# mLSTM scan and feed-forward on one core: queries, keys and state as three bfloat16 parts in 120-row stacks that go through memory, from chunk 7 on

## The chip, the cores and the metric

The program runs on one core of a Trainium2 chip. The metric is the device time of one execution in microseconds, taken as the median of several runs.

## What is computed

For 4 batches and 8 heads, 768 tokens of 40 channels go through a gated matrix memory; its output, 3072 tokens of 320 channels, goes through a feed-forward layer with 2048 hidden units. Cut to what matters:

```python
for t in range(S):                                   # S = 768, D = 40
    m_new = np.maximum(f_gate[:, :, t] + m, i_gate[:, :, t])
    f_stab = np.exp(f_gate[:, :, t] + m - m_new)
    i_stab = np.exp(i_gate[:, :, t] - m_new)
    C = f_stab * C + i_stab * outer(v_t, k_t)         # 40 x 40 per batch and head
    n = f_stab * n + i_stab * k_t
    y[:, :, t] = sigmoid(o_gate_t) * (C @ q_t) / max(|n . q_t|, 1)
h = x @ w_in                                         # x: y as 3072 x 320
g = np.maximum(h, 0.0) + alpha * np.minimum(h, 0.0)
out = g @ w_out                                      # 3072 x 320
```

All inputs and the output are float32.

## The kernel before

**Chunks.** The scan is done in 24 chunks `n` of 128 tokens (6 per batch, `c = n % 6`), all 8 heads at a time. Within a chunk the kernel forms scores K·Q for each head (tile `pS`), multiplies them by decays `E`, and multiplies the result by the values (`pH`). What earlier chunks of the batch left is added from the state `C`, 40 rows (key channel) by 42 columns (values, two columns for the normalizer) per head: `from_state` (tile `pI`, line 299). `update_steps` (tile `pu`, line 151) adds a chunk's keys times values to the state.

**Steps.** `stage_a(n)` transposes the chunk's queries (`pq`) and keys (`pk`) so that channels stand on partitions (`transposed`, line 173, two heads per transpose in 104 rows: one head in rows 0 to 39, the other in rows 64 to 103), splits them into parts, updates the state and splits the values. `stage_b(n)` makes the two halves of the scores (even heads, odd heads), then state part, values and gates. `attention` weaves `stage_a(n+1)` with `stage_b(n)`. Chunks 0 to 6 use plain float32 (`NDIR = 7`).

**Parts.** From chunk 7 on, `stacked` makes a high and a low part, each in float32r (a form of float32 that one pass of the PE takes): ACT copies the high part out of PSUM (`qh`, `kh`, line 181), DVE or POOL subtracts (`ql`, `kl`, lines 183 and 185), and SP issues six copies of 40 rows (line 189) for the queries and six for the keys that lay the parts under each other in a stack of 120 rows (`qS`, `kS`). One matmul per head over the 120 rows then sums high·high, high·low and low·high (line 357). The state product uses the unsplit queries `qf` in float32, two heads at a time: the state tile has the even heads in rows 0 to 39 and the odd heads in rows 64 to 103, zeros elsewhere, so one matmul of 84 columns serves a pair.

**Feed-forward.** Twelve groups of 256 tokens (`FeedForward`): per pair of hidden tiles 16 matmuls of 256 columns into `ph` (lines 487 to 494), ACT and DVE apply the slope, ACT and POOL split the result (`gh`, `gl`, lines 509 and 510), 12 matmuls of 320 columns into `po` (line 518), two pairs later.

**Order.** Each engine runs its instructions in a fixed order. The program writes attention steps between feed-forward steps (`side.until`, 13 steps per group of two chunks); a scheduler in the framework then places every instruction on its engine, so a change of one part can move its neighbours. SP issues nearly all DMAs from one queue, in order: a DMA whose wait is not over holds back all behind it. Loads of `q`, `k`, `v` (`qn`, `kn`, `va`) and of the decay rows (`Lb`) are issued there two chunks ahead.

Of the kernel before, what the change touches and what calls it, by code (L numbers as in the profile page):

```python
# [17 lines left out]
def kernel(ctx: ExitStack, tc: tile.TileContext, q, k, v, i_gate, f_gate, o_gate, w_in, w_out, alpha, out):  # L18
# [54 lines left out]
    qn_t = [const.tile([P, H, 64], F32, tag=f"qn{i}", name=f"qn{i}") for i in range(NQ)]  # L73
    kn_t = [const.tile([P, H, 64], F32, tag=f"kn{i}", name=f"kn{i}") for i in range(NQ)]
# [4 lines left out]
    ones = const.tile([BH, R], F32, tag="ones", name="ones")  # L79
    eT = const.tile([P, NC, BH], F32, tag="eT", name="eT")  # L80
    gamB = const.tile([P, BH, NC], F32, tag="gamB", name="gamB")

    C_t = [const.tile([P, H, VA], F32, tag=f"C{i}", name=f"C{i}") for i in range(3)]
    L_d = dram.tile([BH, S], F32, tag="L_d", name="L_d")

    def load_qk(n):
        b, c = divmod(n, NC)
        t0 = c * P
        nc.sync.dma_start(qn_t[n % NQ][:, :, :D], q[b, :, t0 : t0 + P, :].rearrange("h p d -> p h d"))
        nc.sync.dma_start(kn_t[n % NQ][:, :, :D], k[b, :, t0 : t0 + P, :].rearrange("h p d -> p h d"))  # L90
# [34 lines left out]
    def weighed(n):  # L125
# [4 lines left out]
            kd, kn_t[n % NQ][:, :, :D], wT[:, c, b * H : (b + 1) * H].unsqueeze(2).broadcast_to([P, H, D]), ALU.mult  # L130
# [8 lines left out]
    def update_steps(n):  # L139
# [9 lines left out]
        for h in range(H):  # L149
            r = slice(64 * (h % 2), 64 * (h % 2) + D)  # L150
            nc.tensor.matmul(pu3[r, h], kd[:, h], va[:, h], start=True, stop=True)
        yield
        old, new = C_t[(n - 1) % 3], C_t[n % 3]
# [15 lines left out]

    def transposed(ps, src):  # L170
# [4 lines left out]
    def stacked(ps, nm, n, low, copy=None):  # L175


        X = sb.tile([3 * D, 2, 512], F32R, tag=f"{nm}S", name=f"{nm}S{n}")
        Xh = sb.tile([P, 512], F32R, tag=f"{nm}h", name=f"{nm}h{n}", bufs=1)
        Xl = sb.tile([P, 512], F32R, tag=f"{nm}l", name=f"{nm}l{n}", bufs=1)  # L180
        nc.scalar.copy(Xh[:R], ps[:R])
        if copy is not None and n in QLP:
            nc.gpsimd.tensor_tensor(Xl[:R], copy[:R], Xh[:R].bitcast(F32), ALU.subtract)
        else:
            nc.vector.tensor_tensor(Xl[:R], ps[:R], Xh[:R].bitcast(F32), ALU.subtract)
        for par in range(2):
            for j in range(3):
                src = (Xl if j == low else Xh)[64 * par : 64 * par + D]
                nc.sync.dma_start(X[j * D : (j + 1) * D, par].bitcast(F32), src.bitcast(F32))
# [899 lines left out]
```

## Time and profile before

| what | value |
|---|---|
| median of 3 runs | 517.41 us (514.90 to 520.62) |
| the profiled execution's own time | 514.52 us |
| its span | 512.8 us |
| mean granted PE clock | 0.992 of full |
| busy: PE, PE weight load | 494.3 us (96%), 479.7 us (94%) |
| busy: DVE, ACT, POOL | 338.5 us (66%), 306.3 us (60%), 242.0 us (47%) |
| DMA | 59.43 MB, 140,078 packets |

How to read it: PE is the matmul row, PEld its weight loads, which run beside matmuls. A matmul's row shows how long it is in flight; matmuls overlap, so what one costs is the distance from its start to the start of the next. A row of the timeline gives start and length in us, then engine, source line, operation, output tile <- input tiles, shapes and how many equal instructions it merges; in brackets the idle time before it and what ended it. "SPq" rows are SP issuing a DMA: their length is the time of issuing, not of the transfer. A float32 matmul appears as two records, since PE takes two passes over it; float32r and bfloat16 matmuls and transposes appear as one.

### The profile page before, as it was taken

Reading aid. Unit: us, or ns where it says so; the run is one execution under the profiler, and the core shown is the slowest. Engines: PE = TensorE matmul, PEld = TensorE weight load, DVE = VectorE, ACT = ScalarE, POOL = GpSimd, SP = SyncE. Lnnn points to the kernel's source line nnn. Section 1 sums busy time; section 2 is a strip of 40 time slices with the busy share of each in tenths; the row PEclk is TensorE's granted clock in tenths of the full one; section 3 lists DMA queues with packets and bytes.
Section 4 is the critical chain, followed back from the end, with each engine's and each line's share of the span. In section 5 each row is a group of like instructions: output and inputs, shape, how many; then the busy total and the mean of one; then the engine's idle time right before and its main releaser. Section 6 shows DMA issues by size and latency. Waiting matters only on the chain.

```text
span 512.8 us, 11517 instructions
## 1 busy us (share of the span) xinstructions
PE 494.3 (96%) x4319; PEld 479.7 (94%) x4319; DVE 338.5 (66%) x666; ACT 306.3 (60%) x635; POOL 242.0 (47%) x284
## 2 busy tenths in 40 slices
PE   8887999899999999999999999999999999999997
PEld 7766998889999999999899999998999999999996
DVE  7887999945544777773876667685686586552321
ACT  3768797753456566576785676567776563433332
POOL 6522334400267366564747556464765644333242
PEclk9997999999999999999999999999999999999999
DMA  9989996811175454367363464448343221000000
GB/s 170 229 180 260 256 242 171 170 27 38 60 175 132 117 145 109 99 168 147 85 167 109 116 144 117 119 119 179 102 126 91 71 71 41 1 27 0 27 1 26
DMA packets 140078, 59.43 MB, mean 116 GB/s; under 512 B 102824, under 2 KB 128440, under 8 KB 140024
## 3 DMA queue, kind: packets, MB, share of 16 engines
q1 hardware_dynamic: 139944, 58.61, 47.5%
q8 instruction: 34, 0.56, 0.5%
q14 instruction: 20, 0.16, 0.1%
q10 hardware_dynamic: 80, 0.11, 0.1%
HBM read 37.95 MB, written 4.03 MB: 82 GB/s over the span
## 4 chain that ended last, share of the span: by engine, by line
PE 75%; DVE 11%; DMA 4%; ACT 3%; issue 3%; SPq 2%; POOL 1%; ACTq 0%; DVEq 0%; POOLq 0%
PE po L518 28%; PE ph L487 4%; PE ph L494 4%; PE ph L488 4%; PE ph L490 4%; PE ph L491 4%; PE ph L489 4%; PE ph L492 4%; PE ph L493 4%; PE pI L299 3%; PE pH L282 3%; PE pS L357 2%; DMA og<-in_o_gate_dram 2%; SPq L112 1%; PE pk L173 1%
## 5 line engine op out<-in xcount | busy, mean ns | idle before, releaser
L510 POOL TENSOR_TENSOR gl<-g,gh 128x512 fp32r<-128x512 f32 x80 | 103.9, 1299 | 75.8 <-ACT gh L509 64.2
L518 PE MATMUL po<-OH,gh 128*128 128x320 f32 x384 | 116.3, 315 | 3.2 <-ACT gh L509 2.9
L518 PE MATMUL po<-OL,gh 128*128 128x320 f32 x384 | 113.9, 309 | 0.0
L500 DVE SCALAR_TENSOR_TENSOR g<-g,oma,ph 128x256 f32<-128x256 f32 x160 | 69.6, 476 | 64.4 <-ACT g L496 64.0
L496 ACT ACTIVATE g<-ph 128x512 f32<-128x512 f32 x96 | 57.5, 599 | 65.3 <-PE ph L494 51.6
L509 ACT CAST gh<-g 128x512 fp32r<-128x512 f32 x80 | 49.6, 620 | 52.5 <-DVE g L500 51.8
L518 PEld LDWEIGHTS po<-OH,gh 128*128 128x128 f32 x384 | 71.9, 188 | 4.4 <-ACT gh L509 3.6
L518 PE MATMUL po<-OH,gl 128*128 128x320 f32 x384 | 73.0, 312 | 0.0
L518 PEld LDWEIGHTS po<-OL,gh 128*128 128x128 f32 x384 | 72.0, 188 | 0.0
L346 ACT ACTIVATE E<-Lb,bT 128x128 f32<-128x128 f32 x176 | 54.6, 391 | 16.9 <-PE pH L282 12.8
L518 PEld LDWEIGHTS po<-OH,gl 128*128 128x128 f32 x384 | 59.6, 188 | 0.4 <-POOL gl L510 0.3
L487 PE MATMUL ph<-XH,WH 128*128 128x256 f32 x192 | 59.0, 307 | 0.3 <-DVE g L500 0.2
L488 PE MATMUL ph<-XH,WH 128*128 128x256 f32 x192 | 54.2, 282 | 0.0
L494 PE MATMUL ph<-X2L,W 128*128 128x256 f32 x192 | 54.1, 283 | 0.0
L489 PE MATMUL ph<-XH,WL 128*128 128x256 f32 x192 | 54.1, 282 | 0.0
L490 PE MATMUL ph<-XH,WL 128*128 128x256 f32 x192 | 53.9, 281 | 0.0
L491 PE MATMUL ph<-X,W 128*128 128x256 f32 x192 | 53.9, 281 | 0.0
L492 PE MATMUL ph<-XL,WH 128*128 128x256 f32 x192 | 53.8, 280 | 0.0
L493 PE MATMUL ph<-XL,WH 128*128 128x256 f32 x192 | 53.6, 279 | 0.0
L269 ACT CAST E<-pS 128x512 bf16<-128x512 f32 x64 | 37.5, 586 | 21.1 <-DVE pS L267 10.9
L349 POOL TENSOR_SCALAR_AFFINE_SELECT E<-E 128x512 f32<-128x512 f32 x44 | 30.6, 697 | 31.7 <-ACT E L346 22.8
L487 PEld LDWEIGHTS ph<-XH,WH 128*128 128x128 f32 x192 | 36.3, 189 | 1.2 <-DVE g L500 0.5
(168 smaller groups left out, 1095.9 us busy)
## 6 DMA issues: line engine op xcount, KB each, us to landing
Lb<-L_d SPq DMA_DIRECT2D x22, 512.0 KB
qS<-qh SPq DMA_DIRECT2D x68, 80.0 KB
kS<-kh SPq DMA_DIRECT2D x68, 80.0 KB
wo<-in_moe_w_out_dram SPq DMA_DIRECT2D x8, 640.0 KB
wi<-in_moe_w_in_dram SPq DMA_DIRECT2D x8, 512.0 KB
qn<-in_q_dram SPq DMA_DIRECT2D x24, 160.0 KB
kn<-in_k_dram SPq DMA_DIRECT2D x24, 160.0 KB
va<-in_v_dram SPq DMA_DIRECT2D x24, 160.0 KB
```

The lines of the kernel that those rows point to most:

```text
L487: nc.tensor.matmul(dst, WH[half][:, 0, hs], XH[:, 0], start=True, stop=False)
L488: nc.tensor.matmul(dst, WH[half][:, 1, hs], XH[:, 1], start=False, stop=False)
L489: nc.tensor.matmul(dst, WL[half][:, 0, hs], XH[:, 0], start=False, stop=False)
L490: nc.tensor.matmul(dst, WL[half][:, 1, hs], XH[:, 1], start=False, stop=False)
L491: nc.tensor.matmul(dst, W2[:, fs], X2, start=False, stop=False)
L492: nc.tensor.matmul(dst, WH[half][:, 0, hs], XL[:, 0], start=False, stop=False)
L493: nc.tensor.matmul(dst, WH[half][:, 1, hs], XL[:, 1], start=False, stop=False)
L494: nc.tensor.matmul(dst, W2[:, fs], X2L, start=False, stop=True)
L496: nc.scalar.activation(gt, ph, AF.Relu, scale=-1.0)
L500: nc.vector.scalar_tensor_tensor(out=y[:, e], in0=gt[:, e], scalar=oma[:, f : f + 1], in1=ph[:, e], op0=ALU.mult, op1=ALU.add)
L510: (nc.vector if g < 2 else nc.gpsimd).tensor_tensor(gl, y, gh.bitcast(F32), ALU.subtract)
L518: nc.tensor.matmul(po[j], x[:, e, j * P : (j + 1) * P], W[f // NB][:, f % NB], **ends)
```

## The change

- **Transposes.** The q and k tiles are one tile `qk` without padding for chunks from 7 on; three heads (120 columns) are transposed at a time, so 3 transposes for the queries and 3 for the keys instead of 4 and 4. (The last key transpose starts early and repeats a head, so that it has 120 columns too.)
- **Parts.** Each of q and k becomes three bfloat16 parts: `by_channel_parts` copies the first part out of PSUM on ACT and subtracts on DVE, for queries and then keys; `stacks` makes the second part (ACT) and the third (POOL) for both together.
- **Stacks through memory.** SP writes all parts to a buffer in memory (`parts`, 3 DMAs of 40 rows), then reads back the query stack `Q` (2 DMAs) and the key stack `K` (4 DMAs), each 120 rows in two layers: six products of parts in two matmuls.
- **Scores.** Two bfloat16 matmuls per head instead of one float32r matmul.
- **State.** In batches 1 to 3 the state stands in 40 rows for all heads and is updated in place: POOL decays it, DVE adds `pu`, then ACT, DVE, ACT and POOL make its three bfloat16 parts, and SP issues 3 copies that stack them. `from_state` takes the query stack as weights, two matmuls of 42 columns per head. All eight `pu` matmuls of these chunks write rows 0 to 39; before, even heads wrote rows 0 to 39 and odd heads rows 64 to 103.
- **Order.** The last step of `stage_b(n)` is written ahead of the last of `stage_a(n+1)`, from n = 5 on. `ones`, `qf` (from chunk 7) and the tiles of the old parts are gone.

The float32 scores of chunks 0 to 6 and the float32 state of batch 0 stay. The diff, cut to its core:

```diff
+    parts_d = [dram.tile([2, 3 * D, 9 * P], BF16, tag=f"parts{i}", name=f"parts{i}") for i in range(NQ)]
...
-            r = slice(64 * (h % 2), 64 * (h % 2) + D)
-            nc.tensor.matmul(pu3[r, h], kd[:, h], va[:, h], start=True, stop=True)
+            r0 = 64 * (h % 2) if b == 0 else 0
+            nc.tensor.matmul(pu3[r0 : r0 + D, h], kd[:, h], va[:, h], start=True, stop=True)
         yield
+        if b > 0:
+            state(n, pu3[:D])
+            yield
+            return
...
+    def state(n, pu):
+        b, c = divmod(n, NC)
+        C = C_t[0][:D]
+        if c == 0:
+            nc.vector.tensor_copy(C, pu)
+        else:
+            nc.gpsimd.tensor_tensor(C, C, gamB[...].broadcast_to([D, H, VA]), ALU.mult)
+            nc.vector.tensor_tensor(C, C, pu, ALU.add)
+        X = state_parts(n)
...
+        nc.scalar.copy(X[:D, 0], C)
+        nc.vector.tensor_tensor(rest, C, X[:D, 0], ALU.subtract)
+        nc.scalar.copy(X[:D, 1], rest)
+        nc.gpsimd.tensor_tensor(low, rest, X[:D, 1], ALU.subtract)
+        nc.sync.dma_start(X[D : 2 * D], X[:D])
+        nc.sync.dma_start(X[2 * D : 3 * D, 1], X[:D, 0])
+        nc.sync.dma_start(X[2 * D : 3 * D, 0], low)
...
+    def by_channel_parts(n, j, S, rest):
+        ps = psa(f"p{'qk'[j]}{n}")
+        for i in range(3):
+            c0 = min(j * H * D + 3 * D * i, 2 * H * D - 3 * D) if j else 3 * D * i
+            nc.tensor.transpose(ps[: 3 * D, i * P : (i + 1) * P], flat_t[n % NQ][:, c0 : c0 + 3 * D], ident)
+        nc.scalar.copy(S[: 3 * D, j, 0], ps[: 3 * D, : 3 * P])
+        nc.vector.tensor_tensor(rest[: 3 * D, j], ps[: 3 * D, : 3 * P], S[: 3 * D, j, 0], ALU.subtract)
+
+    def stacks(n, S, rest):
+        nc.scalar.copy(S[: 3 * D, :, 1], rest[: 3 * D])
+        nc.gpsimd.tensor_tensor(S[: 3 * D, :, 2], rest[: 3 * D], S[: 3 * D, :, 1], ALU.subtract)
+        d = parts_d[n % NQ]
+        by_slot = d.rearrange("j (k c) (r x) -> r c j k x", c=D, r=3)
+        for r in range(3):
+            nc.sync.dma_start(by_slot[r], S[r * D : (r + 1) * D])
+        Q, K = (sb.tile([3 * D, 2, 9 * P], BF16, tag=f"{x}S", name=f"{x}S{n}") for x in "qk")
+        row = [slice(i * D, (i + 1) * D) for i in range(3)]
+        by_part = d.rearrange("j (k c) x -> j c k x", c=D)
+        nc.sync.dma_start(Q[: 2 * D], d[0, : 2 * D].unsqueeze(1).broadcast_to([2 * D, 2, 9 * P]))
+        nc.sync.dma_start(Q[row[2]], by_part[0][:, 0:3:2])
+        for i in range(2):
+            nc.sync.dma_start(K[row[i]], by_part[1][:, 0:2])
+        for s in range(2):
+            nc.sync.dma_start(K[row[2], s], d[1, row[2 * (1 - s)]])
...
+            by_channel_parts(n, 0, S, rest)
+            yield
+            by_channel_parts(n, 1, S, rest)
+            Q, K = stacks(n, S, rest)
...
+            C = state_parts(n - 1)[: 3 * D]
+            for h in range(H):
+                es = slice(h * VA, (h + 1) * VA)
+                for s in range(2):
+                    nc.tensor.matmul(pI[:, es], Q[:, s, place(h, False)], C[:, s, es], start=s == 0, stop=s == 1)
...
-                    nc.tensor.matmul(pS[:, sl], K[:, par, sl], Q[:, par, sl], start=True, stop=True)
+                    h = 2 * p + par
+                    for s in range(2):
+                        nc.tensor.matmul(
+                            pS[:, sl], K[:, s, place(h, True)], Q[:, s, place(h, False)], start=s == 0, stop=s == 1
+                        )
...
-            for part in (a, bb, late, a, bb, a, bb):
+            for part in (a, bb, late, a, bb) + ((a, bb) if n + 1 < NC else (bb, a)):
```

**How it moves instructions on SP.** The first place is the issue of the key stack of one chunk in SP's queue, in the middle of the program. Before (rows by source line, operation, tiles and shape; `kS` is the stack, `kh` and `kl` the parts):

```order
L189 DMA kS_2906<-kh_2907 40x512 x2
L189 DMA kS_2906<-kl_2908 40x512
L189 DMA kS_2906<-kh_2907 40x512 x2
L189 DMA kS_2906<-kl_2908 40x512
L90 DMA kn_77<-in_k_dram 128x8x40
L96 DMA va_79<-in_v_dram 128x8x40
L103 DMA Lb_3437<-L_d 128x8x128
```

With the change, for chunk 11 (`parts` is the buffer in memory, `S_11` the parts, `qk` the token-major tile of q and k):

```order
L205 DMA C_85<-cw_2592 40x336
L93 DMA qk_76<-in_k_dram 128x8x40
L234 DMA parts_88<-S_11_2649 40x6x384 x3
L238 DMA qS_2742<-parts_88 80x2x1152
L239 DMA qS_2742<-parts_88 40x2x1152
L241 DMA kS_2743<-parts_88 40x2x1152 x2
L243 DMA kS_2743<-parts_88 40x1152 x2
L93 DMA qk_75<-in_q_dram 128x8x40
```

The six copies inside the chip that each of the stacks took have become three writes and six reads of one buffer, in one block, with the next loads queued behind the reads.

**On PE.** The second place is the state product of a chunk, on PE. Before (`pI` is the product, `qf` the float32 queries, `C` the state):

```order
L518 MATMUL po_1_2329<-OH_1179,gl_6_2718 128x320
L299 MATMUL pI_2804<-C_86,qf_2298 128x84 x4
L282 LDWEIGHTS E_0_2647
L282 MATMUL pH_0_2812<-vb_2463,E_0_2647 128x126
L282 LDWEIGHTS E_0_2647
```

With the change, the end of it for chunk 10 (sixteen pairs of the first two rows stand there in all, then come the values, `pH`):

```order
L367 LDWEIGHTS qS_2397
L367 MATMUL pI_2844<-C_84,qS_2397 128x42
L343 LDWEIGHTS E_0_2694
L343 MATMUL pH_0_2864<-vb_2600,E_0_2694 128x126
L343 LDWEIGHTS E_0_2694
```

Four float32 matmuls of 84 columns have become sixteen bfloat16 matmuls of 42 columns, each with a weight load of its own.

More of the change, by code (lines that the diff above doesn't have):

```diff
@@ L173, in transposed @@
             nc.tensor.transpose(ps[:R, p * P : (p + 1) * P], src[:, p * P : p * P + R], ident)
[L175 to L189, printed above, removed]
-        return X
+    def by_channel_parts(n, j, S, rest):
[5 more added lines that the diff above has]
+        nc.vector.tensor_tensor(rest[: 3 * D, j], ps[: 3 * D, : 3 * P], S[: 3 * D, j, 0], ALU.subtract)
@@ L192, with place @@
+    def place(h, keys):
+        block, slot = (2, h - 5) if keys and h >= 2 * 3 else divmod(h, 3)
+        return 3 * slot + block
     kpads = []
@@ L454 @@
     XNP = range(2, 8)
-    QLP = range(6, 24)
     KDP = range(1, 24)
@@ L850, in first_group @@
         lf = [
-            sb.tile([P, 512], F32, tag="qk"[j] + "h", name=f"g_lf{j}", bufs=1)[:BH, : (GT, S - GT)[j]] for j in range(2)
+            sb.tile([P, 512], F32, tag=f"sp{j}", name=f"g_lf{j}", bufs=1)[:BH, : (GT, S - GT)[j]] for j in range(2)
         ]
```

70 lines of the change are left out of this document (41 added, 29 removed).

## The prediction

> **What bounds the kernel now.** I read the page first (busy times, slices, chain of waits), then the table of stages, then the waits around the scores, then single starts in the timeline.
>
> From the page:
>
> ```profile
> PE 494.3 (96%) x4319; PEld 479.7 (94%) x4319; DVE 338.5 (66%) x666; ACT 306.3 (60%) x635; POOL 242.0 (47%) x284
> PE 75%; DVE 11%; DMA 4%; ACT 3%; issue 3%; SPq 2%; POOL 1%; ACTq 0%; DVEq 0%; POOLq 0%
> ```
>
> From the table of stages (busy time of each engine in each stretch):
>
> ```profile
> 125.00:440.00 315.00, 312.85 (x2851) 307.22 (x2850) 213.55 (x418) 198.77 (x421) 176.16 (x197) 1.00 0.45 115
> 440.00:512.80 72.80, 69.12 (x546) 68.81 (x544) 23.47 (x52) 23.51 (x41) 24.14 (x20) 0.99 0.04 15
> ```
>
> PE is the bound. Between 125 and 440 us, where chunks 7 to 23 go through the parts, it is busy 312.85 of 315 us while DVE, ACT and POOL have 213.55, 198.77 and 176.16; behind 440 only feed-forward is left. So what counts is how much PE work the change takes away, and whether PE gets something to wait for. From the answer on the score tile `pS`, with all waits of PE for it in the whole run:
>
> ```profile
> L357 PE MATMUL pS<-qS,kS x136: 223/274/309, 142.4 to 440.6; 120*128 120x128 f32 x136
>   ACT qf L218: 2.3, 1
> ```
>
> The one wait there is for `qf`, in a direct chunk. For a stack PE never waits now: every one is there in time. That cover is what the change spends.
>
> **PE work, part by part.** Starts in the timeline give what each kind costs PE:
>
> ```profile
> 274.20 0.46 PEld L173 LDWEIGHTS pk<-ident,kn 128*104 128x104 f32 x4
> 278.39 0.56 PE L357 MATMUL pS<-qS,kS 120*128 120x128 f32 x4
> 278.88 0.51 PE L151 MATMUL pu<-va,kd 128*40 128x42 f32 x16
> 279.31 0.39 PE L487 MATMUL ph<-XH,WH 128*128 128x256 f32 x1
> 283.06 1.02 PE L299 MATMUL pI<-C,qf 104*128 104x84 f32 x8
> 283.92 1.10 PE L282 MATMUL pH<-vb,E 128*128 128x126 bf16 x24
> 284.87 0.37 PE L487 MATMUL ph<-XH,WH 128*128 128x256 f32 x1
> 304.50 0.56 PE L357 MATMUL pS<-qS,kS 120*128 120x128 f32 x4
> 304.89 0.33 PE L487 MATMUL ph<-XH,WH 128*128 128x256 f32 x1
> ```
>
> *bfloat16 matmuls.* The values are the nearest kind: 128x128 bfloat16 weights and 126, 84 or 42 columns in turn; 24 take 283.92 to 284.87, 39.6 ns each with their weight loads. From the lengths of two of the three forms,
>
> ```profile
> L282 PE MATMUL pH<-vb,E 128*128 128x126 bf16 x120 | 17.1, 217 | 0.0
> L282 PE MATMUL pH<-vb,E 128*128 128x42 bf16 x120 | 15.7, 183 | 1.2 <-DVE E L270 1.2
> ```
>
> a column costs (217 - 183) / 84 = 0.40 ns, so by estimate 42 columns cost 39.6 - 42 x 0.40 = 23 ns and 128 columns 57 ns.
>
> *State product.* 15 chunks use it (7 to 11, 13 to 17, 19 to 23). Now 283.92 - 283.06 = 0.86 us. With the change sixteen of 42 columns: 0.37 at 23 ns, 0.63 if each cost 39.6. I take 0.40 (25 ns): 15 x (0.40 - 0.86) = **-6.9 us**, bounds -7.4 and -3.4.
>
> *Transposes.* Four weight loads take 0.46 us, 0.115 each. Two fewer in each of queries and keys would be 8 against 6: 17 x 2 x 0.115 = **-3.9 us**; at worst the three wider ones cost what four do, 0.
>
> *Scores.* Four heads now take 0.49 (278.39 to 278.88) or 0.39 us (304.50 to 304.89), mean 0.44; eight of 57 ns take 0.46. 34 halves x 0.02 = **+0.7 us**, bounds -1.0 and +2.4.
>
> *State update.* Sixteen records, eight heads, take 0.43 us (278.88 to 279.31). Even heads write rows from 0, odd heads rows from 64, and these pairs run beside each other. Rows of a split update, six heads and then a lone one:
>
> ```profile
> 332.83 0.43 PE L151 MATMUL pu<-va,kd 128*40 128x42 f32 x12
> 333.19 0.38 PE L487 MATMUL ph<-XH,WH 128*128 128x256 f32 x1
> 372.85 0.27 PE L151 MATMUL pu<-va,kd 128*40 128x42 f32 x2
> 373.05 1.12 PE L299 MATMUL pI<-C,qf 104*128 104x84 f32 x8
> ```
>
> Six heads 0.36, eight 0.43: a pair adds 0.07, and 0.15 is paid once. With all heads in rows 0 to 39 no two run together, so 8 x 0.07 + 0.15 = 0.71 us: 15 x 0.28 = **+4.2 us**. Bounds: 0 (pairing was worth nothing) and eight times the lone head's 0.20, 15 x 1.17 = +17.6.
>
> Sum on PE: -6.9 - 3.9 + 0.7 + 4.2 = **-5.9 us**; by the bounds together -12.3 to +16.6, where the upper end needs every head alone.
>
> **What PE will wait for.** From the last key transpose of a chunk its stacks now need this. By rows of the same work:
>
> ```profile
> L403 ACT CAST XH<-p 128x512 fp32r<-128x512 f32 x11 | 6.5, 590 | 2.5 <-PE p L384 1.6 <-PE ph L490 0.8
> L404 ACT CAST X<-p 128x256 fp32r<-128x256 f32 x11 | 4.2, 384 | 0.2
> L407 DVE TENSOR_TENSOR X2L<-p,X 128x256 fp32r<-128x256 f32 x11 | 4.6, 415 | 0.0
> L406 DVE TENSOR_TENSOR XL<-p,XH 128x512 fp32r<-128x512 f32 x11 | 7.6, 687 | 8.5 <-ACT XH L403 8.5
> L613 ACT CAST OH<-t_wo 128x640 fp32r<-128x640 f32 x8 | 5.8, 721 | 1.3 <-DVE t_wo L605 1.3
> L510 POOL TENSOR_TENSOR gl<-g,gh 128x512 fp32r<-128x512 f32 x80 | 103.9, 1299 | 75.8 <-ACT gh L509 64.2
> ```
>
> 1. Making the parts: ACT 120x384 0.49 and DVE 0.55 (midway between their 256 and 512), ACT 120x768 0.85 (0.72 x 768 / 640), POOL 120x768 1.9 (1.30 x 1.5): 3.8 us.
> 2. Standing in line on those engines. Of this step before, two first copies:
>
> ```profile
> 274.30 0.60 PE L173 MATMUL pk<-ident,kn 128*104 128x128 f32 x4
> 277.93 0.61 ACT L181 CAST kh<-pk 104x512 fp32r<-104x512 f32 x1
> 291.19 0.61 PE L173 MATMUL pk<-ident,kn 128*104 128x128 f32 x4
> 291.84 0.59 ACT L181 CAST kh<-pk 104x512 fp32r<-104x512 f32 x1 [1.54 <-PE pk L173]
> ```
>
> 0.65 us from the transposes' start without a wait, 3.63 with one: up to 3.0 at that engine alone, then POOL with 1.3 us per `gl` ahead. I take 1.2 in all, bounds 0.3 and 3.0.
> 3. The DMAs. Rows of SP:
>
> ```profile
> L189 SPq DMA_DIRECT2D kS<-kl x34: 706/708/1132, 138.9 to 426.0; - x34
> 374.94 0.71 SPq L189 DMA_DIRECT2D kS<-kl  x1
> 377.85 0.42 PE L357 MATMUL pS<-qS,kS 120*128 120x128 f32 x2
> 300.74 0.40 SPq L90 DMA_DIRECT2D kn<-in_k_dram  x1
> 304.55 0.72 POOL L129 TENSOR_TENSOR kd<-kn,wT 128x320 f32<-128x320 f32 x1 [2.10 <-DMA kn<-in_k_dram]
> ```
>
> A copy of 40 rows holds SP 0.71 us. From start of issue to use, the tightest stack copy has at most 2.9 us, and a load from memory for which POOL waited took 3.8. Three writes: the last starts 2 x 0.71 behind the first and lands 2.9 later, 4.3 us. Only then may SP start the reads, since each reads what all three wrote. Six reads: 5 x 0.71, and 3.4 (midway) to land: 7.0 us. Bounds: 3.8 + 6.0 (2.4 us per landing, half a microsecond under the ceiling of 2.9) and 5.2 + 7.4.
>
> Sum: 3.8 + 1.2 + 4.3 + 7.0 = **16.3 us**, bounds 13.9 and 19.4. Before, the keys made one hop and half the queries' work was done earlier; now both go through two hops and wait for the keys.
>
> The Trainium skill (page "DMA: Bandwidth & Descriptors", section "Latency and other measured facts") speaks against such a second hop too: it gives HBM access 0.2 us on average and up to 2 us at high load. By it the two landings could cost some 3.6 us more, an estimate that would make the chain 19.9 us; the `kn` row's 3.8 us bears the order of size out, and no row of before shows a read behind a write of the same buffer in this stretch.
>
> What covers the chain is PE's work between these transposes and the chunk's first score matmul. The rows of that stretch I counted in the new order, feed-forward at the paces of
>
> ```profile
> 280.12 0.28 PE L493 MATMUL ph<-XL,WH 128*128 128x256 f32 x1
> 280.24 0.28 PE L494 MATMUL ph<-X2L,W 128*128 128x256 f32 x1
> 281.30 0.31 PE L518 MATMUL po<-OH,gh 128*128 128x320 f32 x1
> 281.45 0.31 PE L518 MATMUL po<-OL,gh 128*128 128x320 f32 x1
> ```
>
> 0.12 and 0.15 us, the rest at the costs above. Chunk 11, for instance, has 42 `ph`, 48 `po` (12.0 us), 24 values, 16 state products, 8 scores and 6 transposes (2.6): 14.6 us. For chunks 7 to 23: 22.5, 16.3, 13.8, 18.0, 14.6, 16.5, 15.1, 14.0, 15.7, 15.2, 17.2, 13.7, 17.2, 13.8, 18.1, 14.1, 16.9 us. Against a chain of 16.3 nine of 17 fall short, by 16.7 us together; against 13.9 by 0.3, against 19.4 by 60. So **+16.7 us**, bounds 0 and +60. A stall here is not given back: the next chunk's transposes mostly stand behind the waiting scores, and so does the feed-forward whose 12 and 16 matmuls follow in PE's queue. On SP, the loads of the chunk after next stand behind reads that wait for the writes; they have a chunk's time (some 18 us, 315 us for 17) in hand.
>
> The rest is hidden by PE: the state's three parts and the extra `rest` work add some 2 us per chunk to ACT and POOL together, which have 116 and 139 us free in that stretch. If that cover were gone, it would cost 17 x 2 = 34 us.
>
> Total: 514.5 (this execution) - 5.9 + 16.7 = 525.3 us. The median of the runs lies 2.9 us above the profiled execution; I add half of that and take **527 us**.
>
> **The rivals.**
>
> *The stacks come in time* (faster). If the landings are short and the engines free, the chain is 13.9 and no chunk waits: 514.5 - 5.9 + 0.3 + 1.5 = 510 us, down to 504 at the lower bounds of the PE terms. For it: nothing of SP is tight before, and 2.9 is a ceiling. Against it: it needs both hops near the lower ends and POOL free each time. It decides once the chain is below about 14.8 us, where stalls (5 us) fall under the PE gain. Chance 0.19.
>
> *Gain and stalls cancel.* At a chain of 15.2 the shortfall is 7 us: 514.5 - 5.9 + 7 + 1.5 = 517 us. Chance 0.19.
>
> *PE pays for weight loads openly.* If a bfloat16 load, up to the 23 ns of the smallest matmul, is not hidden behind its matmul, the 272 score matmuls cost 80 ns: +6.3 us, so 533 with the forecast's stalls. The values' 39.6 ns speak against it. The Trainium skill ("TensorE: Matmul & The Clock Gate", section "Back-to-back issue gap") gives about 81 ns as the sustained distance at 128 columns, which is this case; its time is the same 533 us, and the value rows don't bear it out. Chance 0.05.
>
> *SP's queue becomes the limit.* If landings take 3.8 and loads fall behind too, 19.4 us of chain: 514.5 - 5.9 + 60 = 569 at its bound, about 545 halfway. Chance 0.12.
>
> **How the numbers follow.** The forecast, waits for the stacks on about half the chunks, has 0.45. Over 1% (about what a measurement of this kernel can tell from no change; 5.2 us) slower: 0.45 + 0.05 + 0.12 = 0.62; within: 0.19; faster: 0.19. The likeliest case's own range is 521 to 538. The range for 8 in 10 takes in half of the faster case and half of the SP case: 508 to 543 us.
>
> **What would show it.** Right: PE idle ahead of the first score matmul, ended by a DMA of `kS`, 1 to 4 us on many chunks; PE busy time lower; `pu` at 0.7 us per update, `pI` at 0.4; 16 us from the key transposes to the last landing. Wrong: no waits at `pS` (the chain is short), or waits elsewhere, such as `po` for `gl` behind POOL's new work.

## The result, and the profile after

With the change the kernel takes 559.01 us (median of 4 runs, 553.48 to 565.46) where the kernel before takes 516.59 (4 runs): a ratio of 1.077, with a 95% interval of 1.066 to 1.088. The profiled execution took 559.01 us as well, with a span of 557.3. The forecast was 527 us, in a range of 508 to 543. The direction was right, but the time lies above the range, and the loss is four times as large as forecast: 42.4 us instead of 10.

From the page of the changed kernel, its busy times, its chain of waits, and the group of score matmuls (behind the second bar stands the idle time ahead of the group, and what ended most of it):

```profile
PE 510.0 (92%) x4541; PEld 487.9 (88%) x4541; DVE 355.0 (64%) x681; ACT 320.0 (57%) x667; POOL 267.4 (48%) x300
PE 40%; DMA 24%; DVE 9%; POOL 7%; issue 7%; SPq 6%; ACT 6%; ACTq 0%; POOLq 0%
L427 PE MATMUL pS<-qS,kS 120*128 120x128 bf16 x272 | 25.3, 231 | 26.5 <-DMA kS<-parts 18.1
```

And from its table of stages (columns as before: PE, PEld, DVE, ACT, POOL, granted clock, DMA share, GB/s):

```profile
125.00:440.00 315.00, 287.45 (x2692) 275.96 (x2691) 200.04 (x379) 188.74 (x401) 175.32 (x186) 0.96 0.59 145
```

PE has fallen from 75% to 40% of the chain that ends last, and the DMAs have 24%. Ahead of the scores, where PE waited for no stack before, it now stands idle for 26.5 us, 18.1 of them put down to the key stack's DMAs. Between 125 and 440 us it is busy 287.45 us instead of 312.85. The clock column says something else that the prediction nowhere counts: 0.96 where 1.00 stood.

Where the 44.5 us between the two profiled executions lie can be read from the starts of all matmuls. A distance of over 0.35 us between two starts is idle time (less 0.15 for the matmul itself); half the time under half clock is lost; the rest is PE's own work:

| up to the last matmul, us | PE's own work | idle | lost at half clock | sum |
|---|---|---|---|---|
| before | 488.6 | 15.8 | 3.0 | 507.4 |
| after | 483.5 | 49.8 | 18.9 | 552.2 |
| difference | -5.1 | +34.0 | +15.9 | +44.8 |

Some 5 us of the last column fall before 60 us, where the change touches nothing: half clock took 6.8 us there in the execution before and 20.5 in the one after, and it lies between these two values in all 16 traces of this case. From 60 us on, half clock goes from none to 23.9 us. PE stands idle for some 3.5 of them, so some 10 us are lost there.

### The profile page after: what moved, and what is told of

The parts are those of the page before. It is cut to its first block, busy times and chain, and to the rows that moved or that the text cites. A ratio compares the mean times of both kernels' runs of the same rounds, so it can differ in the third digit from the quotient of the medians.

```text
span 557.3 us, 11903 instructions
## 1 busy us (share of the span) xinstructions
PE 510.0 (92%) x4541; PEld 487.9 (88%) x4541; DVE 355.0 (64%) x681; ACT 320.0 (57%) x667; POOL 267.4 (48%) x300
## 4 chain that ended last, share of the span: by engine, by line
PE 40%; DMA 24%; DVE 9%; POOL 7%; issue 7%; SPq 6%; ACT 6%; ACTq 0%; POOLq 0%
PE po L589 15%; DMA kS<-parts 10%; DMA parts<-S 8%; POOL S L230 3%; DMA Lb<-L_d 2%; PE pS L427 2%; PE warm L915 2%; PE ph L559 2%; PE ph L563 2%; PE ph L561 2%; PE ph L564 2%; PE ph L566 2%; PE ph L560 2%; PE ph L565 2%; PE ph L562 2%
## 5 line engine op out<-in xcount | busy, mean ns | idle before, releaser
L589 PE MATMUL po<-OH,gh 128*128 128x320 f32 x352 | 108.4, 320 | 0.7 <-ACT OH L684 0.7
L589 PE MATMUL po<-OL,gh 128*128 128x320 f32 x352 | 106.1, 314 | 0.0
L589 PE MATMUL po<-OH,gl 128*128 128x320 f32 x352 | 69.0, 317 | 0.0
L589 PEld LDWEIGHTS po<-OH,gh 128*128 128x128 f32 x352 | 67.2, 192 | 1.1 <-ACT OH L684 0.9
L589 PEld LDWEIGHTS po<-OL,gh 128*128 128x128 f32 x352 | 67.1, 191 | 0.1
L589 PEld LDWEIGHTS po<-OH,gl 128*128 128x128 f32 x352 | 55.6, 191 | 0.1
L565 PE MATMUL ph<-XL,WH 128*128 128x256 f32 x192 | 55.3, 288 | 0.0
L561 PE MATMUL ph<-XH,WL 128*128 128x256 f32 x192 | 55.1, 287 | 0.0
L564 PE MATMUL ph<-XL,WH 128*128 128x256 f32 x192 | 55.0, 287 | 0.0
L562 PE MATMUL ph<-XH,WL 128*128 128x256 f32 x192 | 54.9, 286 | 0.0
L230 POOL TENSOR_TENSOR S<-Sr,S 120x768 bf16<-120x768 f32 x17 | 28.2, 1657 | 52.4 <-ACT S L229 52.4
L427 PE MATMUL pS<-qS,kS 120*128 120x128 bf16 x272 | 25.3, 231 | 26.5 <-DMA kS<-parts 18.1
```

What stands on the lines that cost most here:

```text
L561: nc.tensor.matmul(dst, WL[half][:, 0, hs], XH[:, 0], start=False, stop=False)
L562: nc.tensor.matmul(dst, WL[half][:, 1, hs], XH[:, 1], start=False, stop=False)
L564: nc.tensor.matmul(dst, WH[half][:, 0, hs], XL[:, 0], start=False, stop=False)
L565: nc.tensor.matmul(dst, WH[half][:, 1, hs], XL[:, 1], start=False, stop=False)
L589: nc.tensor.matmul(po[j], x[:, e, j * P : (j + 1) * P], W[f // NB][:, f % NB], **ends)
```

## The experiments

Three questions: how much comes from PE's wait for the stacks, how much from the DMAs that nobody on PE waits for, and what the half clock is. Ratios are to the kernel before, run on the same chip.

**No wait for the stacks.** The scores read a constant tile; all parts, writes and reads stay. The scores are meaningless; the rest of the work is the same.

```diff
-    pS[:, sl], K[:, s, place(h, True)], Q[:, s, place(h, False)], start=s == 0, stop=s == 1
+    pS[:, sl], x[: 3 * D, :P], x[: 3 * D, P : 2 * P], start=s == 0, stop=s == 1     # x: ident as bfloat16
```

> This kernel is the change with one thing taken away: the score matmuls of the chunks from 7 on read the identity tile instead of the two stacks (same shapes, same number), so PE waits for no stack there; parts, writes and reads of the stacks all stay. Its scores are therefore not those of the reference. Theory (PE waits for stacks that come late, and its clock is halved after each long wait): the 26.5 us of idle time ahead of the scores go, and the 24 us at half clock between 125 and 490 us (12 us lost) go too; what is left is the PE gain of 6 us against before: 511 to 521 us. Rival (the extra DMA traffic and the extra work of ACT, DVE and POOL slow the whole program, the scores only show it first): the idle time turns up at other instructions and the time stays above 540 us.

Measured: 532.17 us, ratio 1.028 (1.020 to 1.036). Between the two expectations: by the ratios some 26 us of the loss come with this wait, but about 15 us remain although PE waits for no stack at all. From the waits of this kernel (total, times, longest):

```profile
PE p L457 <- DVE xn L398: 6.1, 4, 2.4
PE pH L343 <- DVE XL L479: 5.7, 1, 5.7
...
ACT S L222 <- DMA parts<-S: 17.7, 6, 4.6
ACT L125 <- DMA og<-in_o_gate_dram: 7.0, 2, 6.3
...
POOL kd L138 <- DMA qk<-in_k_dram: 14.1, 5, 5.5
```

ACT waits 17.7 us until the writes have read the one buffer of the parts, and 7.0 for the gates of the next batch; POOL waits 14.1 for keys. These end with a DMA, on which PE does not wait itself. PE's 5.7 us for `XL` stand behind ACT's 6.3 us for the gates, and the six gate loads stood in SP's queue behind a state copy whose issue took 4.1 us:

```profile
235.56 4.07 SPq L204 DMA_DIRECT2D C<-C  x1
...
241.29 4.61 SPq L121 DMA_DIRECT2D og<-in_o_gate_dram  x6
```

Not every wait here is a DMA's doing: 2.3 us of PE's 6.1 for `xn`, at 402 us, come behind a DVE product that took 3.15 us beside POOL's work, the new third part among it (see the last section). That wait is there with half of the bytes, too.

**Half the bytes read back.** Only one of the two layers of each stack is read, and both matmuls use it (so products are repeated and others left out).

```diff
-        nc.sync.dma_start(Q[: 2 * D], d[0, : 2 * D].unsqueeze(1).broadcast_to([2 * D, 2, 9 * P]))
+        nc.sync.dma_start(Q[: 2 * D, 0], d[0, : 2 * D])
```

The other reads are cut in the same way; five of one layer each remain.

> The change with only the first of the two layers of each stack read back from memory (552 KB per chunk instead of 1106, five DMAs instead of six); both score and state matmuls of a head use that layer, so the second layer's products are left out and the first's counted twice. Theory A (the reads' transfer sets the landing): from the last issue to the scores it falls from 5.6 to about 3.5 us, the chain from the key transposes from 17.3 to about 14.8, the idle time ahead of the scores from 26.5 to about 5 us, and the time to 521 to 532 us. Theory B (a fixed latency sets the landing): the chain falls by less than 0.7 us, idle time stays above 20 us, the time above 548 us.

**Key transposes and stacks in the first step** of `stage_a`, so that more of PE's work lies between them and the scores; the computation is whole.

```diff
             by_channel_parts(n, 0, S, rest)
-            yield
             by_channel_parts(n, 1, S, rest)
             Q, K = stacks(n, S, rest)
+            yield
```

> The change with the key transposes, and all that follows them up to the stacks, written into the first step of a chunk's preparation, right behind the query transposes, instead of the second. The whole computation stays. By the new order PE has 14.5 to 24 us of other work between the last transpose and the scores (before the move 13.6 to 18). Theory (lead against chain): three of 17 chunks fall short of 17.3 us, by 5 us together; idle ahead of the scores falls to about 5 us, half-clock time in that stretch to under 8: 518 to 533 us. Rival (the chain grows with the lead, since loads, the one buffer of the parts or SP's queue are late as well): idle stays above 15 us and the time above 540 us.

Measured: 530.19 us, ratio 1.021 (1.014 to 1.029), and 531.54 us, ratio 1.027 (1.019 to 1.035). PE's wait for the key stack falls from 18.1 us to 8.0 (half the bytes) and 3.8 (early):

```profile
PE pS L426 <- DMA kS<-parts: 8.0, 8, 1.5
```

```profile
PE pS L427 <- DMA kS<-parts: 3.8, 5, 2.4
```

With half the bytes the stacks come about 4 us behind the last read's issue where PE waits, instead of 5.0 to 6.4. Both times are as the first theory of each has them, and both kernels stop where the first experiment stopped. Not every sign came: PE's idle time ahead of the scores is 8 to 9 us in both, not 5, and the early kernel has 10.2 us of half clock between 125 and 490 us, not under 8.

**What is left: DMAs or engines?** All nine stack DMAs are gone; scores and state product read the constant tile; ACT, DVE and POOL still make all parts.

```diff
-        for r in range(3):
-            nc.sync.dma_start(by_slot[r], S[r * D : (r + 1) * D])
...
+        return None, None
```

> As the run whose scores read a constant tile, and the nine stack DMAs of each chunk are gone as well (the state product reads the constant tile too); ACT, DVE and POOL still make all parts, the state's three copies stay. That run took 532 us against 517 of before, with no wait for a stack. Theory A (what is left of the loss comes from the DMAs: the ACT copy that waits until the writes have read the parts, 17.7 us there, and SP's queue, in which the gate loads stand behind writes that wait): 510 to 517 us, no ACT wait for the writes, no 6 us gap of PE at a batch's start. Rival B (the added work and the changed order on ACT, DVE and POOL cost it): 526 to 533 us, with PE waits of 10 us and more on engines in the stretch of chunks 7 to 23.

Measured: 516.49 us, ratio 0.997 (0.993 to 1.001). Theory A: without the stack DMAs the loss is gone. But PE's saved work doesn't show as a gain either, so the added work on the other engines may cost the few microseconds that PE saves. Then the writes alone were put back:

```diff
+        for r in range(3):
+            nc.sync.dma_start(by_slot[r], S[r * D : (r + 1) * D])
```

> The run without any stack DMA (ratio 0.997 to before) with the three writes per chunk put back, the six reads still gone and scores and state product reading a constant tile. Theory A (what is left of the loss in the run with all stack DMAs, ratio 1.028, comes from SP waiting, ahead of the first read, until the writes have landed, with the loads, gates and state copies queued behind): without reads SP never waits for a landing, ratio 0.99 to 1.005. Rival B (the single buffer of the parts: ACT's next copy waits until the writes have read it): that wait stays, ratio 1.012 to 1.03. Rival C (the bytes of the reads): as A here.

Measured: 520.04 us, ratio 1.005 (1.001 to 1.008). The reads, or the wait ahead of them, make up most of the rest. To take the wait away, the writes were left out from the third of these chunks on, so that reads fetch old bytes (base: the first experiment):

```diff
-        for r in range(3):
+        for r in range(3 if n < NDIR + NQ else 0):
             nc.sync.dma_start(by_slot[r], S[r * D : (r + 1) * D])
```

> The run whose scores read a constant tile (ratio 1.028) with the writes done for the first two chunks only: every later chunk's reads fetch these old bytes, 1.1 MB per chunk as before, but wait for no write. Theory A (SP's wait for the landing): ratio 0.99 to 1.01. Rival C (the reads' bytes, which slow the loads, or the place they take in the DMA queues): ratio 1.02 to 1.03.

Measured: 537.53 us, ratio 1.039 (1.035 to 1.044), worse than with the wait, which neither theory had. Its waits:

```profile
SPq L238 <- PE pI L367: 31.0, 8, 8.1
...
POOL kd L138 <- DMA qk<-in_k_dram: 31.4, 5, 13.3
...
PE po L590 <- POOL gl L582: 17.5, 3, 9.7
```

Free of the writes, the scheduler set reads of later chunks ahead in SP's queue. There they waited for a stack buffer until the state product (`pI`) had read it, the keys' load stood behind them, POOL stood still for the keys 13.3 us, and PE for POOL's `gl` 9.9 and 7.5 us, in two places. So this run did not tell the wait from the bytes. It shows two other things: what a DMA that waits does to an in-order queue, and that bytes alone need not cost much: behind the second gap, at 232 us, 1.11 MB per chunk were read on, and the distance to the kernel before grew no more (25 us there, 23 at the end, with some 3 us of PE's saved work in it).

Then the bytes were halved under the constant tile, by the edits of the first two experiments together. SP's wait for the writes stays (43.0 us in all, up to 4.3 at a time):

> The run whose scores read a constant tile (full reads, ratio 1.028) with half of the stacks' bytes read back (0.55 MB per chunk instead of 1.1). SP still waits for the writes to land ahead of the first read, ACT still waits for the single buffer of the parts. Theory C (the reads' bytes hold up SP's queue and what is behind it): ratio 0.998 to 1.010, and SP's issues over 1 us fall from 17 to about 9, as before. Theory A (SP's wait for the landing, whatever the bytes): ratio 1.018 to 1.030.

Measured: 519.73 us, ratio 1.006 (1.003 to 1.009). The time is as theory C has it, so the hold alone, whatever the bytes, is not what costs. The second sign of theory C did not come: 16 of SP's issues between 125 and 440 us still take over 1 us, though they sum to 22.6 us instead of 49.8 and the longest is 2.2 instead of 4.5. The same waits as above, in this run:

```profile
ACT S L222 <- DMA parts<-S: 7.7, 3, 4.0
...
POOL kd L138 <- DMA qk<-in_k_dram: 7.3, 6, 2.3
...
PE p L456 <- DVE xn L397: 3.7, 3, 2.4
```

And early transposes and half the bytes together, again by the edits above:

> Key transposes in the first step and half of the stacks' bytes read back, together; each alone gave a ratio of 1.027 and 1.021 with 9 us of PE idle ahead of the scores left. If the rest in each is still mainly the stacks' lateness, the two together leave less than 3 us of idle there and a ratio of 1.000 to 1.012. If the rest is the same blocking that the run with a constant tile has, the idle ahead of the scores goes but the ratio stays at 1.018 to 1.028.

Measured: 520.44 us, ratio 1.003 (0.998 to 1.007), with 0.8 us of PE idle left ahead of the scores. The first expectation held. The steps from kernel to kernel now make a ladder:

| stack DMAs per chunk | does PE wait for them | ratio |
|---|---|---|
| none | no | 0.997 |
| 3 writes | no | 1.005 |
| 3 writes, half the reads | no | 1.006 |
| 3 writes, half the reads | yes, early transposes | 1.003 |
| 3 writes, half the reads | yes | 1.021 |
| 3 writes, all reads | no | 1.028 |
| 3 writes, all reads | yes, early transposes | 1.027 |
| 3 writes, all reads (the change) | yes | 1.077 |

The tables of stages of the runs without a wait for the stacks (none, half, all), 125 to 440 us:

```profile
125.00:440.00 315.00, 311.58 (x3060) 301.61 (x3059) 224.69 (x434) 211.80 (x450) 198.58 (x211) 1.00 0.29 68
```

```profile
125.00:440.00 315.00, 309.01 (x3022) 297.80 (x3021) 220.17 (x427) 209.28 (x447) 197.83 (x211) 0.99 0.50 126
```

```profile
125.00:440.00 315.00, 300.22 (x2898) 288.50 (x2897) 214.02 (x411) 202.75 (x438) 190.26 (x205) 0.98 0.63 151
```

A mean DMA share of 0.63 is no full queue, and yet PE loses 9 us more than at 0.50. The share comes in bursts: SP holds the reads until the writes have landed, then 1.11 MB go off at once, and the loads and the next writes stand behind them. Over single microseconds the share passes 0.9 in 29 of 100 with all reads and in 20 with half. That the bursts are the cause fits these runs; their length was not varied alone.

**Two single suspects.** The sigmoid of the next batch's gates, for which ACT waits at a batch's start, was moved one chunk on, in the early kernel and under the constant tile:

```diff
             load_gate(b + 1, nc.sync)
-            open_gate(b + 1)
...
+        elif b > 0:
+            open_gate(b)
```

> The kernel with the key transposes in the first step (531.5 us), with one thing moved: the sigmoid of the next batch's gates no longer stands in ACT's queue right behind the last chunk of a batch but ahead of the first use, one chunk later. Theory (at three batch starts ACT waits for the gate loads that stand behind the stacks in SP's queue, and PE behind ACT; the gap at 249 us was 2.45 us): 526 to 529 us, no ACT wait for the gates. Rival (these waits are cover for others, PE then waits for the stacks instead): 530 to 533 us.

> The run whose scores read a constant tile (ratio 1.028, a 5.9 us gap of PE at the start of batch 2 behind an ACT wait of 6.3 us for the gate loads), with the sigmoid moved to one chunk later. Theory (the gate loads behind the blocked stack DMAs are the largest part of what is left): the 12 us step at that batch start is gone, ratio 1.000 to 1.012. Rival (the loss moves to other waits): ratio 1.02 to 1.03.

Measured: 531.85 us, ratio 1.028 (1.020 to 1.035), and 531.73, ratio 1.026 (1.021 to 1.032). No gain, and the times are those of the rivals. But the traces show that neither run tested the suspect: the scheduler put the sigmoid at the same place of ACT's queue as before, between the same neighbours. Under the constant tile, without the edit and with it:

```profile
242.03 0.62 ACT L581 CAST gh<-g 128x512 fp32r<-128x512 f32 x1
248.94 1.28 ACT L125 ACT_TABLE_LOAD   x1 [6.29 <-DMA og<-in_o_gate_dram]
...
251.94 0.57 ACT L476 CAST XH<-p 128x512 fp32r<-128x512 f32 x1
```

```profile
243.93 0.62 ACT L582 CAST gh<-g 128x512 fp32r<-128x512 f32 x1
251.41 1.28 ACT L125 ACT_TABLE_LOAD   x1 [6.85 <-DMA og<-in_o_gate_dram]
...
254.41 0.57 ACT L477 CAST XH<-p 128x512 fp32r<-128x512 f32 x1
```

PE's longest single wait in these two runs, 5.7 and 6.2 us, stands behind this one, and in the first of them half clock for two windows behind it. With half of the bytes ACT waits 1.7 us there, as long as in the kernel before (1.8). What a sigmoid at another place would gain stays open.

And the state's three copies, issued by ACT instead of SP, in the early kernel:

```diff
-        nc.sync.dma_start(X[D : 2 * D], X[:D])
+        nc.scalar.dma_start(X[D : 2 * D], X[:D])
```

> The kernel with the key transposes in the first step (531.5 us), with the state's three copies per chunk (0.72 us of SP each, up to 4.0) issued by ACT instead of SP. Theory (SP's queue, full of stack DMAs, delays stacks and loads): the chain of the late chunks gets 2 us shorter and the time is 524 to 529 us. Rival (the landing of the stacks' bytes sets the chain, not SP's issue): 530 to 536 us, with ACT 30 us busier in issue and PE's wait for the stacks about as before.

Measured: 536.47 us, ratio 1.038 (1.032 to 1.045). No gain, and the time is just past the rival's range: the chain from the key transposes to the scores is 23.5 us in the mean (with time that PE did not wait) against 23.7, so SP's own issues were not what made it long.

**Filling the wait.** Matmuls were put ahead of the scores, to use the wait and to keep the clock up: sixteen on the query stack in eight chunks, then ten on a constant tile in all chunks.

```diff
+            if par == 0 and n in (7, 8, 10, 14, 16, 18, 20, 22):
+                for _ in range(16):
+                    nc.tensor.matmul(pS[:, : 2 * P], Q[: 2 * D, 0, 0], Q[: 2 * D, 0, :2], start=True, stop=True)
```

```diff
+            if par == 0 and n >= NDIR:
+                x = ident.bitcast(BF16)
+                for _ in range(10):
+                    nc.tensor.matmul(pS[:, : 2 * P], x[:, :P], x, start=True, stop=True)
```

> The change, with sixteen matmuls of 256 columns (0.11 us each, 1.8 us together) ahead of the first scores of chunks 7, 8, 10, 14, 16, 18, 20 and 22, the ones that waited longest. They work on the part of the query stack that lands first, and the scores overwrite their result. PE has something to do in the last two microseconds of the wait. Theory (the half clock follows from idle PE): the time at half clock between 125 and 490 us falls from 24 us to under 8, the idle time ahead of the scores falls by about 10, and the time falls by some 8 us to about 551, although 14 us of matmuls were added. Rival (the clock falls for another reason, or the extra matmuls push the rest): half-clock time stays at 20 us or more and the time is 559 or up to 14 us longer.

> The changed kernel (559.0 us) with ten bfloat16 matmuls of 256 columns on a constant tile (1.07 us) ahead of each chunk's scores, 18.2 us of PE work in all. Theory (the clock is halved in the 3.41 us window behind one in which PE was idle for more than about 1.9 us): the waits take up about 13 us of it, the half clock between 125 and 480 us falls from 23.8 us to 7 or less, and the time is 549 to 557 us although 18 us of work came in. Rival (half clock comes by something other than idle time): it stays above 17 us, and the time is 563 us or more.

Measured: 570.92 us, ratio 1.104 (1.095 to 1.114), and 568.83, ratio 1.097 (1.087 to 1.106). Neither theory held, and the signs of both rivals came: the filling was added to the time, and half clock from 60 us on stayed at 23.9 us in both. But the wait was not filled. In the second run PE still waited for the key stack, and longer at a time:

```profile
PE pS L431 <- DMA kS<-parts: 19.8, 10, 3.5
```

In the nine chunks where PE waited for over 1 us, 4 to 79 other matmuls stood between the fill and the scores; in the other eight the fill stood right ahead of them and there was hardly a wait (0.3 us at most). And the fill took the place of feed-forward work that the scheduler then put elsewhere: in chunks 8, 16, 18, 20 and 22 PE's own work between key transposes and scores is 13.7 to 16.4 us with the fill of 1 us in it, and 14.4 to 16.4 in the changed kernel. So these runs do not decide on the reading of the clock below.

**A version that gains.** If lateness and bytes are all that is wrong, PE's saved work should show once both are gone. Two parts in place of three: one layer, one matmul per head for scores and state product, early transposes, no third part.

```diff
-                    for s in range(2):
-                        nc.tensor.matmul(pS[:, sl], K[:, 0, place(h, True)], Q[:, 0, place(h, False)], start=s == 0, stop=s == 1)
+                    nc.tensor.matmul(pS[:, sl], K[:, 0, place(h, True)], Q[:, 0, place(h, False)], start=True, stop=True)
```

> Two parts in place of three: the products with a third part and second by second are left out, so the sums have fewer bits. One layer is read back (0.55 MB per chunk), one matmul per head for scores and for the state product, no third part on POOL, two state copies on SP, and the key transposes in the first step. Theory (the rest of the loss is lateness and bytes; PE work pays where nothing waits): against the run with early transposes and half the bytes (ratio 1.003) PE loses another 136 x 0.057 + 120 x 0.025 = 10.8 us, so a ratio of 0.978 to 0.992. Rival (PE work no longer sets the time in these chunks; another engine or the loads do): 0.995 to 1.010.

Measured: 506.75 us, ratio 0.977 (0.973 to 0.981), just past the fast end of what the theory gave.

```profile
125.00:440.00 315.00, 311.93 (x2909) 301.75 (x2907) 229.15 (x449) 216.81 (x462) 163.68 (x185) 1.00 0.46 114
```

PE is busy 311.93 of 315 us again, at full clock. Its own work is 474.6 us up to the last matmul, 14.0 less than before; the 10.8 of its expectation and the 5.1 of the change would have made 15.9.

## Why the prediction was right in direction and wrong in size

**PE's work: right within its noise.** -5.9 us forecast, -5.1 measured. From the timeline of the changed kernel:

```profile
269.25 0.81 PE L160 MATMUL pu<-va,kd 128*40 128x42 f32 x16
269.99 0.41 PE L589 MATMUL po<-OH,gh 128*128 128x320 f32 x1
...
305.54 0.62 PE L427 MATMUL pS<-qS,kS 120*128 120x128 bf16 x8
306.00 0.56 PE L367 MATMUL pI<-C,qS 120*128 120x42 bf16 x16
306.40 0.36 PE L559 MATMUL ph<-XH,WH 128*128 128x256 f32 x1
```

By the starts, the state update takes 0.74 us (0.71 forecast), eight score matmuls 0.46 (0.46), the state product 0.40 (0.40), and three transposes 0.25 where four took 0.36, 3.7 of the forecast 3.9 us. Four scores before took 0.40 in the median, not 0.44, so by these terms alone the gain is nearer 4 us. The total is not sharp: the same reckoning gives -1.6 to -5.5 us for the eleven other traces with the same matmuls (fills and two parts left out). The rival of openly paid weight loads is out. The sign that the prediction named for its own case, "PE busy time lower", was a bad one: the page's busy time rose from 494.3 to 510.0 us, mainly because matmuls under half clock count twice as long.

**The waits for the stacks: the mechanism right, the size wrong.** It is step 3 of the chain, the DMAs, that failed. One chunk, from its key transposes to its scores:

```profile
362.18 0.49 PE L221 MATMUL pk<-ident,qk 128*120 128x128 f32 x3
362.70 0.48 ACT L222 CAST S<-pk 120x384 bf16<-120x384 f32 x1 [0.82 <-PE pk L221]
363.21 0.56 DVE L223 TENSOR_TENSOR Sr<-pk,S 120x384 f32<-120x384 f32 x1 [0.60 <-ACT S L222]
363.93 0.85 ACT L229 CAST S<-Sr 120x768 bf16<-120x768 f32 x1
364.85 1.65 POOL L230 TENSOR_TENSOR S<-Sr,S 120x768 bf16<-120x768 f32 x1 [3.18 <-ACT S L229]
366.53 1.78 SPq L234 DMA_DIRECT2D parts<-S  x3
371.68 0.31 SPq L238 DMA_DIRECT2D qS<-parts  x1
372.04 0.37 SPq L239 DMA_DIRECT2D qS<-parts  x1
372.45 0.73 SPq L241 DMA_DIRECT2D kS<-parts  x2
373.22 0.72 SPq L243 DMA_DIRECT2D kS<-parts  x2
377.11 0.28 PE L559 MATMUL ph<-XH,WH 128*128 128x256 f32 x1
379.95 0.27 PE L427 MATMUL pS<-qS,kS 120*128 120x128 bf16 x1 [2.56 <-DMA kS<-parts]
```

The transposes end at 362.67. The parts are done at 366.50: 3.8 us, as forecast. The first read starts 5.2 us behind the first write's issue (4.3 forecast), and the scores 8.3 behind that (7.0). In the mean of the 17 chunks the third write lands, as far as SP's first read shows it, 3.9 us behind its issue, not 2.9, and the stacks 6.0 behind the last read's issue, not 3.4. Issuing was cheaper than forecast:

```profile
L243 SPq DMA_DIRECT2D kS<-parts x34: 332/342/350, 148.8 to 475.8; - x34
L204 SPq DMA_DIRECT2D C<-C x15: 723/752/3682, 97.4 to 459.1; - x15
```

some 0.34 us each to and from memory, while the 40-row copy inside the chip still costs 0.75; in the mean that took back 2 us (0.9 us from the first write to the third instead of 1.4, 2.0 from the first read to the last instead of 3.6). In the 13 chunks where PE waited, the chain was mostly 16.9 to 18.3 us. Against 17.3 the seventeen leads of the prediction fall short by 28.1 us (17.3 less each lead, where that is positive), and 26.5 to 29.5 us of idle ahead of the scores were measured. The count of the leads was good: PE's own work in each stretch is within 0.9 us of it. One microsecond too little on the chain cost 11 us, since by then nearly every chunk falls short: 13 waited, not nine. That the two sums are so near is in part luck: chunks 7, 8 and 10, with late parts, waited 8.1 us where 1.0 falls short, and chunk 9 not at all where 3.5 does. The sentence on memory access that the prediction quoted from the Trainium skill ("DMA: Bandwidth & Descriptors", section "Latency and other measured facts"), by which the chain would be 19.9 us, was the better hint for the landings: they came 1.0 and 2.6 us later than forecast, together the 3.6 us of that estimate. The chain's mean is 19.0 us, with four chunks above 20 in which the parts alone took 8 to 13 us.

**What the prediction left out: the clock.** Two windows of 3.41 us from the changed kernel's table of stages:

```profile
294.11:297.52 3.41, 0.76 (x9) 0.60 (x10) 1.21 (x2) 1.63 (x4) 3.41 (x5) 0.99 1.12 211
297.52:300.94 3.42, 3.42 (x17) 3.38 (x15) 2.44 (x5) 1.89 (x4) 2.67 (x4) 0.51 0.28 69
```

and two starts from its timeline in the second of them:

```profile
298.25 0.47 PE L589 MATMUL po<-OH,gh 128*128 128x320 f32 x1
298.51 0.47 PE L589 MATMUL po<-OL,gh 128*128 128x320 f32 x1
```

In the first window PE is busy for 0.76 us. In the next it is busy throughout, but at a clock of 0.51, and its `po` matmuls start 0.27 us apart instead of 0.15. A wait of 2.6 us thus costs 1.7 us more behind it. Six stretches make the 23.9 us at half clock, and some 10 us of loss. The prediction's +16.7 us counts the waits alone and puts this at nothing.

**What the prediction called covered, and was not.** It said of the loads behind the waiting reads that they have a chunk's time in hand. In the run with the constant tile 15 us remain, and some 11 of them (1.028 against 1.006) go with half of the reads' bytes. PE mostly does not see it as a wait for a DMA, but as waits for DVE, ACT and POOL, which wait for keys, gates and the parts' buffer. The largest of them that the trace shows is the one batch start with the late gates.

**The sum,** by the ladder: about +26 us for PE's wait on the stacks with its half clock (1.077 against 1.028), +11 for the second half of the reads' bytes (1.028 against 1.006), +4 for the writes and the held queue (1.006 against 0.997), and -1 for all else; together the 40 of the ratio of 1.077. PE's own 5.1 us should have made that last figure -5. Its interval reaches to -3.4, and in that run's trace PE has 2.4 us less of own work than before but 2.7 us more of idle time. The "SP queue" rival of the prediction (545 to 569) had the right end of the range, and in the late loads part of the reason. Its sum came about otherwise: the mean chain is near its 19.4 us, but not half of its 60 us of stalls came.

**What stays open.** Whether holding the queue or the length of the burst is the worse half was not separated at full size, since the one run that took the hold away changed the order. The half clock was read from traces, not tested: neither run meant for it filled the waits. And the sigmoid of the gates, behind whose wait the longest single gap lies, was never moved.

## What to carry to other kernels

A round trip through memory that PE waits for is priced by its landings, and these grow with the bytes that are in flight: 6 us for 1.11 MB here, 4 us for half of it. Compare the chain with each chunk's own cover: a microsecond on a chain that is near the cover costs a microsecond on every chunk, and idle time on PE costs again in clock: here some 10 us of half clock beside 34 us of added idle time. Look in the trace whether an edit moved what it was meant to move: of the runs here, two left the order as it was and two the wait. And before a DMA is made to wait in an in-order queue, list the loads behind it and who needs them; ask for fewer bytes before asking for fewer instructions.

## What the runs showed of the hardware

- **Half clock goes by a fixed grid of 3.41 us.** In every trace the stretches at half clock start on such a grid and last one or more steps. Over the 16 traces, from 60 to 480 us, 36 windows at full clock had 1.9 us or more of PE idle: 35 were followed by half clock. Of 19 windows with 1.7 to 1.9 us, 4 were; of 1854 with less, 3. The Trainium skill ("TensorE: Matmul & The Clock Gate", section "What's actually happening") has the window and the two clocks, but lets the clock fall after an idle window of about 3.4 us; here a little over half a window is enough. A long case, in the run with the constant tile, is a window with no matmul at all and two at half clock behind it:

```profile
248.50:251.90 3.40, 0.00 (x0) 0.00 (x0) 0.00 (x0) 2.95 (x2) 0.00 (x0) 1.00 0.18 33
251.90:255.30 3.40, 1.85 (x16) 1.56 (x16) 2.76 (x6) 2.86 (x7) 0.00 (x0) 0.51 0.00 0
255.30:258.70 3.40, 3.40 (x15) 3.40 (x15) 1.67 (x4) 3.37 (x7) 3.10 (x3) 0.50 0.13 39
```

- **Issuing a DMA can take microseconds.** The same copy (`C<-C`) holds SP 0.75 us as a rule and 3.7 at most; under the constant tile, 17 issues over 1 us sum to 49.8 us.
- **A DVE product of two SBUF tiles was slow beside POOL's work.** In the run with the constant tile one 128x320 `xn` product took 3.15 us, while POOL ran two operations of 1.27 and 1.63 us, and PE waited 2.3 us for it. Over all 16 traces the 62 products with no POOL operation beside them took 0.48 to 0.49 us.
